# Second-level Strassen for one product of layer 1, groups in pairs, and a planned order in a fused attention and mixture-of-experts kernel

## The chip, the cores and the metric

The kernel runs on one core of a Trainium2 chip. The metric is the device time of one execution in microseconds; lower is better. Engines are named as in the profile: PE is TensorE (matmuls; PEld is its weight loads), DVE is VectorE, ACT is ScalarE, POOL is GpSimd, SP is SyncE. PE writes its results to PSUM, eight banks of 512 fp32 columns on each of 128 partitions.

## The reference

Block-sparse attention gives x, and a mixture of eight experts, mixed by weights P that are normalised by rows and columns in turn (Sinkhorn), works on x:

```python
x = np.ascontiguousarray(attn_out.transpose(0, 2, 1, 3)).reshape(B * S, H * D)
...
N, D, E, F = (3072, 512, 8, 1024)
...
P = np.exp(logits)
for _ in range(8):
    P /= P.sum(1, keepdims=True) + 1e-09
    P /= P.sum(0, keepdims=True) + 1e-09
    P *= N / E
out = np.zeros((N, D), dtype=np.float32)
for e in range(E):
    h = np.maximum(x @ w1[e], 0.0)
    ye = h @ w2[e]
    out += P[:, e:e + 1] * ye
```

Every expert is dense: all 3072 rows go through both layers of each of the eight experts.

## The kernel before, in words

**Three stretches.** Attention and expert 0 come first, up to about 124 us. A bridge follows (`bridge`, to about 165 us): the rest of expert 0, the Sinkhorn rounds, and the first layer of the first part of expert 1. Both are ordered by a list planner (`Plan`, lines 36 to 134): each unit has an engine, a cost, dependencies and a priority, and the planner emits, engine by engine, the unit that can start first, and among those within 0.02 the one of lowest priority value. The engines then run what was emitted in that order, waiting on semaphores. The third stretch, 165 us to the end, is a loop written out by hand (lines 1264 to 1313), and this is what the change rewrites.

**Strassen-Winograd.** Experts 1 to 7 compute both layers with seven block products in place of eight. In layer 1 the two row halves of w1 (256 each) and its two column halves are the blocks A, the halves of x (transposed) the blocks B. In layer 2 the hidden h is A and w2 is B. The sums S1 to S4 are formed of A, T1 to T4 of B, on DVE in fp16 (lines 931 to 983).

**A group** `(e, j, i)` (line 997) is one tile of layer 1: expert e, columns 512 j of each half of the 3072 rows (three values of j), hidden features 128 i of each half (four values of i). Its seven products p1 to p7 have two matmuls each, of 512 columns (line 988), and use four PSUM banks in turn: `pa` and `pb` (tag "ab", two banks) and `pg` (tag "g", two banks, so that groups overlap). ACT copies the first product into the bank of the third (seed), puts two partial sums aside (c5, c2) and applies two of the relus (r11, r21); DVE applies the other two with an added operand (c12, c22, line 938). The four results A11, A12, A21, A22 of 512 columns go to a tile `hf`, and four DVE sums s1 to s4 of 512 columns (lines 932 and 935) give S1 to S4 of the second layer in the same tile.

**A pair** `(e, j, c)` (line 1063) is one tile of layer 2: 128 rows ta of the upper half of the output and 128 rows tb of the lower half. Its seven products q1 to q7 have four matmuls of 256 columns each (line 994), and write a tile `xy` of two banks (four parts of 256 columns; two such tiles). c1 (ACT, line 1094), v5 (DVE, line 1099) and v6 (ACT, line 1106) move sums between parts. ya and yb add two parts each, times P, to `out_acc`, 512 columns in one DVE instruction (line 1124).

**The loop.** There are 84 groups and 84 pairs. Step n runs group n beside pair n - 4 (`LAG = 4`), with the products of both in a fixed mixture and the DVE and ACT work between them. The sums of the next expert's weights (`w1_sums`, `w2_sum`) and its loads on POOL's queue (`load_w1`, `load_w2`) are put at fixed steps. The four first groups are in the bridge; the four last pairs form a hand-written tail, two of whose pairs use the "ab" and "g" banks and add in halves of 256 columns (`y_half`, `x_half`).

Of the kernel before, what the change touches and what calls it, by code (L numbers as in the profile page):

```python
# [19 lines left out]
class Unit:  # L20
# [3 lines left out]
    def __init__(self, eng, cost, fn, deps, prio, opens, lag, shape=None):  # L24
        self.eng = eng if isinstance(eng, dict) else {eng: cost}
        self.shape = shape
        self.fn, self.deps, self.prio, self.opens, self.lag = fn, deps, prio, opens, lag
        self.start = self.end = self.on = None

# [6 lines left out]
class Plan:  # L36
# [22 lines left out]
    def order(self):  # L59
# [26 lines left out]
        while waiting or left:  # L86
# [51 lines left out]
def kernel(  # L138
# [778 lines left out]
    if True:  # L917
# [7 lines left out]
        steps = [(e, j) for e in range(1, E) for j in range(NJ)]  # L925
# [71 lines left out]
        def group(e, j, i):  # L997
            h = hs[e, j, i] = fast.tile([128, 7, 512], FP16, tag="hf", name="hf", bufs=8)
            B = {}

            def p1():
                B["a"] = fps.tile([128, 512], FP32, tag="ab", name="pa", bufs=2)
                product1(e, i, j, B["a"], "A11", "B11", True)

            def seed():
                B["g"] = fps.tile([128, 512], FP32, tag="g", name="pg", bufs=2)
                nc.scalar.copy(out=B["g"][:], in_=B["a"][:])  # L1007

            def p5():
                B["b"] = fps.tile([128, 512], FP32, tag="ab", name="pb", bufs=2)  # L1010
                product1(e, i, j, B["b"], "S1", "T1", True)

            def c5():
                B["c5"] = fast.tile([128, 512], FP32, tag="c5", name="c5", bufs=1)
                nc.scalar.copy(out=B["c5"][:], in_=B["b"][:])  # L1015

            def p6():
                product1(e, i, j, B["g"], "S2", "T2", False)

            def c2():  # L1020
                B["c2"] = fast.tile([128, 512], FP32, tag="c2", name="c2", bufs=1)
                nc.scalar.copy(out=B["c2"][:], in_=B["g"][:])  # L1022

            def p2():
                product1(e, i, j, B["a"], "A12", "B21", False)

            def r11():
                relu("ACT", h[:, A11, :], B["a"][:])

            def p3():  # L1030
                product1(e, i, j, B["b"], "S4", "B22", False)

            def c12():
                relu_plus(h[:, A21, :], B["b"][:], B["c2"][:])

            def p7():
                product1(e, i, j, B["g"], "S3", "T3", False)

            def c22():
                relu_plus(h[:, A22, :], B["g"][:], B["c5"][:])  # L1040

            def p4():
                product1(e, i, j, B["g"], "A22", "T4", False)

            def r21():
                relu("ACT", h[:, A12, :], B["g"][:])

            def s1():
                plus(h[:, S1, :], h[:, A21, :], h[:, A22, :])

            def s3():
                sub(h[:, S3, :], h[:, A11, :], h[:, A21, :])

            def s2():
                sub(h[:, S2, :], h[:, S1, :], h[:, A11, :])

            def s4():
                sub(h[:, S4, :], h[:, A12, :], h[:, S2, :])

            return {f.__name__: f for f in (p1, seed, p5, c5, p6, c2, p2, r11, p3, c12, p7, c22, p4,  # L1060
                                            r21, s1, s3, s2, s4)}

        def pair(e, j, c, spare=False, c1_at=None, tail=False):
            def h(q):
                return lambda f: hs[e, j, f][:, q, :]
# [3 lines left out]
            def part(*ks):  # L1069
                if not spare:  # L1070
                    return B["x"][:, ks[0]:ks[-1] + 1:max(1, ks[-1] - ks[0]), :]
                t, k = B["xy"[ks[0] // 2]], ks[0] % 2
                return t[:].rearrange("p (k d) -> p k d", k=2)[:, k:k + 1, :]

            def at(k):
                return part(k)[:, 0, :]

            def scale0():
                for t in (ta, tb):
                    nc.scalar.activation(out=out_acc[:, t, :], in_=out_acc[:, t, :], func=AF.Copy,  # L1080
                                         scale=P_sb[:, t, 0:1])

            def q1():
                if spare:
                    nc.gpsimd.tensor_scalar_mul(out=P_sb[:, tb, 0:1], in0=P_sb[:, tb, e:e + 1], scalar1=-1.0)
                    B["x"] = fps.tile([128, 512], FP32, tag="ab", name="px", bufs=2)
                    B["y"] = fps.tile([128, 512], FP32, tag="g", name="py", bufs=2)
                else:
                    B["x"] = xps.tile([128, 4, DH], FP32, tag="xy", name="xy", bufs=2)
                product2(e, c, at(0), h(A11), "B11", True)  # L1090

            def c1():
                B["c1"] = c1_at if c1_at is not None else fast.tile([128, DH], FP32, tag="c1", name="c1", bufs=1)[:]
# [26 lines left out]
            def add(t, k, *src):  # L1120
                src = part(*src)
                w = src.shape[1]
                acc = out_acc[:, t, k * DH:(k + w) * DH].rearrange("p (h d) -> p h d", h=w)
                nc.vector.scalar_tensor_tensor(out=acc, in0=src, scalar=P_sb[:, t, e:e + 1], in1=acc,  # L1124
# [16 lines left out]
            def fin():  # L1141
                if e == E - 1:
                    between(out_acc[:, tb, 0:DH], out_acc[:, tb, DH:DM], out_acc[:, tb, 0:DH])
                    store(tb)
# [4 lines left out]
            def y_half():  # L1149
                s3 = fast.tile([128, DH], FP32, tag="y3", name="y3", bufs=1)  # L1150
                nc.scalar.activation(out=s3[:], in_=at(3), func=AF.Copy, scale=P_sb[:, ta, e:e + 1])
                add(tb, 1, 2)
                store(tb, slice(DH, DM))
                nc.vector.scalar_tensor_tensor(
                    out=out_acc[:, tb, 0:DH], in0=at(2), scalar=P_sb[:, tb, 0:1],
                    in1=out_acc[:, tb, 0:DH], op0=ALU.mult, op1=ALU.add)
                nc.gpsimd.tensor_tensor(out=out_acc[:, ta, DH:DM], in0=out_acc[:, ta, DH:DM], in1=s3[:], op=ALU.add)

            def x_half():
                add(ta, 0, 0)  # L1160
                store(ta, eng=nc.scalar)
                nc.vector.scalar_tensor_tensor(
# [4 lines left out]
            return {f.__name__: f for f in (scale0, q1, c1, q5, v5, q6, v6, q2, q7, q3, q4, ya, yb, fin, ahead, y_half, x_half)}  # L1167

        def bridge():
            t = [fps.tile([128, 512], FP32, tag="g", name="allg", bufs=2) for _ in range(2)]  # L1170
# [6 lines left out]
            for n in range(8):  # L1177
# [26 lines left out]
                for eng, us, fn, o, w in (("DVE", 0.62, rows, (), ()), ("POOL", 0.7, by_rows, (), ()),  # L1204
                                          ("DVE", 0.48, columns, (), ()), ("PE", 0.12, totals, [buf], ()),
                                          ("DVE", 0.2, inverse, (), [buf]), ("POOL", 0.7, by_columns, (), ())):
                    step = add(eng, us, fn, [step], -50.0, opens=o, uses=w, lag=0.7 if fn is columns else 0.0)

            X, Wt = {}, {}
# [6 lines left out]
            for i in range(4):  # L1216
                for n in range(4):
                    Wt[i, n] = add("DVE", 0.3, lambda i=i, n=n: w1_sum(1, i, n), [Wt.get((i, n - 1)), U["w1n", i]],
                                   980.0 + 5 * i + n)
            step2 = None  # L1220
            for n in range(4):
                step2 = add("DVE", 0.62, lambda n=n: w2_sum(1, n),
                            [step2] + [U["pj", halves[-2], c] for c in range(HG)] + [U["w2n"]], PW + 0.01 * n)
            for i in range(4):
                f = made[1, 0, i] = group(1, 0, i)
                a, b, g = Buffer("ab"), Buffer("ab"), Buffer("g")
                k5, k2 = Buffer("c5"), Buffer("c2")
                d = {}

                def op(name, eng, us, deps, opens=(), uses=()):  # L1230
                    d[name] = add(eng, us, f[name], [d[x] if isinstance(x, str) else x for x in deps],
                                  1000.0 + PRI[i], opens=opens, uses=uses)

                op("p1", "PE", 0.44, [U["w1n", i]], [a])
                op("seed", "ACT", 0.58, ["p1"], [g], [a])
                op("p5", "PE", 0.44, ["p1", Wt[i, 0], X[0, 0]], [b])
# [130 lines left out]
```

## Time and profile before

| | us |
|---|---|
| median of 3 runs | 670.81 (670.65 to 671.78) |
| the profiled execution | 671.95 |
| its span | 670.2 |
| PE busy in 300 to 400 us | 99.92 of 100 |
| DVE busy in 300 to 400 us | 81.49 of 100 |
| ACT busy in 300 to 400 us | 56.72 of 100 |
| first q1 of the loop on PE, start | 164.87 |
| last p4 of the loop on PE, start | 651.21 |
| last instruction on DVE, start | 665.97 |

The page gives for each engine the busy time, its share of the span and the number of instructions. A line of the timeline gives the start and the length in us, the engine, the line of the kernel, the operation, output and input tiles with their shapes, a count of merged instructions, and in brackets the idle time of the engine just before it and what ended that. A matmul's length is longer than the distance to the next one, since matmuls are pipelined; distances between starts are what tells PE's pace. The other engines' instructions overlap a little too.

### The profile page before, as it was taken

The page shows a single profiled execution, that of the slowest core. Times are in us where ns is not written, and L with a number is a line of the kernel's source. Part 1 is how long each engine was busy: PE and PEld are TensorE (multiplying, and loading weights), DVE is VectorE, ACT ScalarE, POOL GpSimd, SP SyncE. Part 2 cuts the span into 40 slices and gives each one's busy share as a digit, 9 for nine tenths or more (in the row PEclk, how much of TensorE's full clock was granted, in tenths as well). Part 3 has the DMA queues.
Part 4 walks back from the last instruction along what each step waited for, and adds up shares of the span by engine and source line. Part 5 has one row for each costly group of instructions (what it writes and reads, how often), then busy time and mean ns, then how long its engine had stood idle before and what let it go on. Part 6 is the DMA issues. An engine that isn't in the chain of part 4 may idle for free.

```text
span 670.2 us, 13349 instructions
## 1 busy us (share of the span) xinstructions
PE 659.3 (98%) x5077; PEld 435.6 (65%) x5077; DVE 549.5 (82%) x1308; ACT 399.6 (60%) x781; POOL 132.4 (20%) x179
## 2 busy tenths in 40 slices
PE   7999999999999999999999999999999999999996
PEld 4666656555666666666666666666666666666665
DVE  7879998775888877888788878887789778987885
ACT  5776766566777765655565556555655565556551
POOL 8599504223001010201010010101020101100001
PEclk9999999999999999999999999999999999999999
DMA  9999958600513050502331051305040132201224
GB/s 161 183 148 146 138 84 85 83 1 2 78 16 33 1 79 1 49 1 40 41 32 16 1 79 17 33 1 79 1 41 9 30 50 24 25 2 56 87 79 158
DMA packets 124032, 36.74 MB, mean 55 GB/s; under 512 B 110144, under 2 KB 121152, under 8 KB 123968
## 3 DMA queue, kind: packets, MB, share of 16 engines
q0 software_dynamic: 104128, 25.93, 40.9%
q1 hardware_dynamic: 18880, 9.22, 6.2%
q8 instruction: 40, 0.66, 0.4%
q10 hardware_dynamic: 960, 0.74, 0.3%
q14 instruction: 24, 0.20, 0.1%
HBM read 52.45 MB, written 6.29 MB: 88 GB/s over the span
## 4 chain that ended last, share of the span: by engine, by line
PE 91%; DVE 5%; DMA 1%; ACT 1%; issue 1%; DVEq 0%; ACTq 0%
PE xy L994 37%; PE pg L988 16%; PE pb L988 11%; PE pa L988 11%; PE yps L233 5%; PE hps L223 5%; DVE xs L549 1%; DMA vx<-in_v_dram 1%; PE sg L385 1%; PE tkq L351 1%; PE ss L472 1%; PE tx L556 1%; PE vs L395 0%; DVE km L379 0%; PE py L994 0%
## 5 line engine op out<-in xcount | busy, mean ns | idle before, releaser
L994 PEld LDWEIGHTS <-hf 128*128 128x128 f16 x2352 | 230.1, 98 | 96.3 <-issue 1.6
L994 PE MATMUL xy<-w,hf 128*128 128x256 f16 x1312 | 183.4, 273 | 0.1
L994 PE MATMUL xy<-ws,hf 128*128 128x256 f16 x984 | 147.6, 273 | 0.2
L214 ACT ACTIVATE hf<-pg 128x512 f16<-128x512 f32 x84 | 50.2, 597 | 150.7 <-PE pg L988 150.7
L1124 DVE SCALAR_TENSOR_TENSOR out_acc<-xy,P_sb,out_acc 128x512 f32<-128x512 f32 x164 | 115.2, 744 | 2.4 <-PE xy L994 2.2
L932 DVE TENSOR_TENSOR hf<-hf 128x512 f16<-128x512 f16 x252 | 99.4, 421 | 9.5 <-ACT hf L214 1.1
L988 PE MATMUL pa<-xT,w 128*128 128x512 f16 x336 | 99.9, 379 | 0.0
L988 PEld LDWEIGHTS <-w 128*128 128x128 f16 x672 | 65.8, 98 | 43.8 <-issue 0.3
L938 DVE CUSTOM_DVE_ANT_0 hf<-pb,c 128x512 f16<-128x512 f32 x84 | 58.0, 691 | 40.4 <-PE pb L988 36.6
L199 POOL DMA_DIRECT2D w<-in_moe_w_dram x56 | 41.8, 758 | 220.6 <-PE pg L988 192.4
L988 PEld LDWEIGHTS <-ws 128*128 128x128 f16 x504 | 49.3, 98 | 24.9
L935 DVE TENSOR_TENSOR xy<-xy,c 128x256 f32<-128x256 f32 x82 | 35.5, 433 | 33.7 <-PE xy L994 32.8
L1022 ACT COPY c<-pg 128x512 f32<-128x512 f32 x84 | 49.2, 586 | 22.7 <-PE pg L988 22.7
L938 DVE CUSTOM_DVE_ANT_0 hf<-pg,c 128x512 f16<-128x512 f32 x84 | 57.2, 680 | 0.7 <-PE pg L988 0.7
L214 ACT ACTIVATE hf<-pa 128x512 f16<-128x512 f32 x84 | 50.6, 602 | 1.3 <-PE pa L988 1.3
L1007 ACT COPY pg<-pa 128x512 f32<-128x512 f32 x84 | 47.9, 570 | 4.7
L988 PE MATMUL pg<-xTs,w 128*128 128x512 f16 x168 | 50.0, 379 | 0.1
L988 PE MATMUL pb<-xT,ws 128*128 128x512 f16 x168 | 50.0, 379 | 0.0
L988 PE MATMUL pg<-xT,w 128*128 128x512 f16 x168 | 50.0, 379 | 0.0
L988 PE MATMUL pb<-xTs,ws 128*128 128x512 f16 x168 | 50.0, 379 | 0.0
L988 PE MATMUL pg<-xTs,ws 128*128 128x512 f16 x168 | 50.0, 379 | 0.0
L1015 ACT COPY c<-pb 128x512 f32<-128x512 f32 x84 | 49.7, 592 | 0.2 <-ACT pg L1007 0.2
(150 smaller groups left out, 796.2 us busy)
## 6 DMA issues: line engine op xcount, KB each, us to landing
w<-in_moe_w_dram POOLq DMA_DIRECT2D x8, 1024.0 KB, 9.2
w<-in_moe_w_dram POOLq DMA_DIRECT2D x56, 128.0 KB, 3.5
out_dram<-out_acc SPq DMA_DIRECT2D x20, 256.0 KB, 2.0
vx<-in_v_dram POOLq DMA_DIRECT2D x16, 192.0 KB, 6.2
qst<-in_q_dram POOLq DMA_DIRECT2D x31, 96.0 KB, 5.3
kst<-in_k_dram POOLq DMA_DIRECT2D x24, 96.0 KB, 5.4
w<-in_moe_w_dram POOLq DMA_DIRECT2D x2, 512.0 KB, 9.4
Ve<-vx SPq DMA_DIRECT2D x48, 10.2 KB, 4.1
```

The source lines that it names most:

```text
L199: nc.gpsimd.dma_start(out=t[:, :, h, :], in_=moe_w1[e].rearrange("(dk p) f -> p dk f", p=128)[:, :, f:f + 128])
L214: nc.scalar.activation(out=out, in_=in_, func=AF.Relu, bias=0.0, scale=1.0)
L223: nc.tensor.matmul(hp[:, 0:n], lhsT=w1s[e][:, dk, 128 * f:128 * (f + 1)], rhs=xT[:, dk, t0:t0 + n], start=(dk == 0), stop=(dk == KD - 1))
L932: nc.vector.tensor_tensor(out=out, in0=in0, in1=in1, op=ALU.subtract)
L935: nc.vector.tensor_tensor(out=out, in0=in0, in1=in1, op=ALU.add)
L938: nc.vector._custom_dve(TENSOR_ADD_SAT, out=out, in0=in0, in1=in1, s0=FLT_MAX, s1=0.0)
L988: nc.tensor.matmul(bank[:], lhsT=w[:, dk, :], rhs=x[:, dk, :], start=start and dk == 0, stop=dk == KH - 1, skip_group_check=True)
L994: nc.tensor.matmul(bank, lhsT=a(f)[:, 128 * c:128 * (c + 1)], rhs=w[:, f, :], start=start and f == 0, stop=f == FH - 1, skip_group_check=True)
L1007: nc.scalar.copy(out=B["g"][:], in_=B["a"][:])
L1015: nc.scalar.copy(out=B["c5"][:], in_=B["b"][:])
L1022: nc.scalar.copy(out=B["c2"][:], in_=B["g"][:])
L1124: nc.vector.scalar_tensor_tensor(out=acc, in0=src, scalar=P_sb[:, t, e:e + 1], in1=acc, op0=ALU.mult, op1=ALU.add)
```

## The change

Three things are changed together, from the end of the attention on.

**Second level for p1.** Two neighbouring groups i = 2u and 2u + 1 become a duo. Their two p1 products (A11 x B11 for 128 features each) together are a product of 256 x 256 by 256 x 512, and are computed by seven pieces m1 to m7 of one matmul with 256 columns each, in the two banks a0 and a1. Two half copies on ACT (sd, c5s) and two joins on DVE (j1, j2) combine them. The sums for it are new: `wa_sum`, four of 128 columns for each duo of an expert, and `xa_sum`, four of 256 columns for each j, once. From (e, j) = (1, 2) on all duos are split; those before keep p1 whole.

**Groups in pairs.** A duo has one `hf` tile of 7 x 2 x 512, and s1 to s4 are one instruction of 1024 columns for both groups. The second layer's tile of two banks becomes two tiles x and y of one bank each, and ya and yb become four adds y0 to y3 of 256 columns, one for each part.

**A planned order.** The hand-written loop and tail are replaced by the planner. `feed(n)` adds the units of a duo, of two pairs two duos back, and the weight loads and sums; priorities come from a table `PR` of one number per kind of unit, plus 100 for each duo. A unit now also waits, in the plan, for all earlier users of its PSUM banks on other engines. PSUM has the same eight banks: two "ab", two "g", two "x", two "y".

```diff
@@ Plan.order
                     t = max([t0, free.get(e, 0.0)]
-                            + [d.end + d.lag + hop(d, e) for d in u.deps])
+                            + [d.end + d.lag + hop(d, e) for d in u.deps]
+                            + [x.end + x.lag + hop(x, e) for b in u.banks for x in b.users
+                               if x.start is not None and x.on != e])
...
+        def moving1a(what, j):
+            t = slice(256 * j, 256 * (j + 1))
+            if what in ("T1", "T2", "T4"):
+                return xa["T1 T2 T4".split().index(what)][:, t]
+            o = 512 * j + (256 if what in ("B12", "T3", "B22") else 0)
+            return xT[:, int(what in ("B21", "B22")), o:o + 256]
...
+        def weight1a(what, e, u):
+            if what in ("S1", "S2", "S4"):
+                return wa[e, u][:, "S1 S2 S4".split().index(what), :]
+            return w1s[e, 2 * u + int(what in ("A21", "S3", "A22"))][:, int(what in ("A12", "A22")), 0, :]
...
-        def group(e, j, i):
-            h = hs[e, j, i] = fast.tile([128, 7, 512], FP16, tag="hf", name="hf", bufs=8)
...
+        def duo(e, j, u):
...
+            def piece(bank, lo, a, b, start=False):
+                nc.tensor.matmul(B[bank][:, lo:lo + 256], lhsT=weight1a(a, e, u), rhs=moving1a(b, j),
+                                 start=start, stop=True, skip_group_check=True)
+            def m1():
+                B["a0"] = psum("ab")
+                piece("a0", 0, "A11", "B11", True)
+            def sd():
+                B["a1"] = psum("ab")
+                nc.scalar.copy(out=B["a1"][:, 0:256], in_=B["a0"][:, 0:256])
+            def m5():
+                piece("a0", 256, "S1", "T1")
+            def c5s():
+                B["m5"] = single("m5", (128, 256), late)
+                nc.scalar.copy(out=B["m5"][:], in_=B["a0"][:, 256:512])
+            def m2():
+                piece("a0", 0, "A12", "B21")
+            def m6():
+                piece("a1", 0, "S2", "T2")
+            def j1():
+                plus(B["a0"][:, 256:512], B["a1"][:, 0:256], B["m5"][:])
+            def m3():
+                piece("a0", 256, "S4", "B22")
+            def m7():
+                piece("a1", 0, "S3", "T3")
+            def j2():
+                plus(B["a1"][:, 256:512], B["a1"][:, 0:256], B["m5"][:])
+            def m4():
+                piece("a1", 0, "A22", "T4")
...
             def s1():
-                plus(h[:, S1, :], h[:, A21, :], h[:, A22, :])
+                plus(h(S1), h(A21), h(A22))
...
-            def ya():
-                add(ta, 0, 0, 3)
...
-            def yb():
-                add(tb, 0, 1, 2)
...
+            def add_to(t, k, src):
+                acc = out_acc[:, t, k * DH:(k + 1) * DH]
+                nc.vector.scalar_tensor_tensor(out=acc, in0=at(src), scalar=P_sb[:, t, e:e + 1], in1=acc,
                                                op0=ALU.mult, op1=ALU.add)
...
+            def y0():
+                add_to(ta, 0, 0)
+            def y1():
+                add_to(tb, 0, 1)
+            def y2():
+                add_to(tb, 1, 2)
+            def y3():
+                add_to(ta, 1, 3)
...
+        us = dict(m=0.1092, p=0.4316, q=0.4368, seed=0.49, c5=0.49, c2=0.49, r=0.49, c12=0.607, c22=0.607, s=0.6,
+                  c1=0.275, v6=0.275, v5=0.34, y=0.665, half=0.275, join=0.34, w1=0.205, w2=0.6, wa=0.14, x=0.6,
+                  xa=0.2, sc=0.62, part=0.34)
+        LAGS = {"ACT": 0.06, "DVE": 0.04}
...
+                op("m1", "PE", us["m"], w[0] + begin + split, [a[0]])
+                op("sd", "ACT", us["half"], ["m1"], [a[1]], [a[0]])
+                op("m5", "PE", us["m"], ["m1"] + t(0), (), [a[0]])
+                op("c5s", "ACT", us["half"], ["m5"], [k5], [a[0]])
+                op("m2", "PE", us["m"], ["sd"], (), [a[0]])
+                op("m6", "PE", us["m"], ["sd"] + t(1), (), [a[1]])
+                op("j1", "DVE", us["join"], ["m6", "c5s"], (), [*a, k5])
+                op("m3", "PE", us["m"], ["j1"] + t(3), (), [a[0]])
+                op("m7", "PE", us["m"], ["j1"] + t(2), (), [a[1]])
+                op("j2", "DVE", us["join"], ["m7"], (), [a[1], k5])
+                op("m4", "PE", us["m"], ["j2"] + w[1], (), [a[1]])
...
-        for n in range(LAG, len(groups)):
...
+                op("y0", "DVE", us["v5"], ["q2"] + old[:1], (), [bx], p=PR["yd"])
+                op("y1", "DVE", us["v5"], ["q4"] + old[1:], (), [bx], p=PR["yd"] + .1)
+                op("y2", "DVE", us["v5"], ["q7"] + old[1:], (), [by], p=PR["yd"] + 2)
+                op("y3", "DVE", us["v5"], ["q3", "y0"] + old[:1], (), [by], p=PR["yd"] + 2.1)
...
+        AHEAD = 3
+        for n in range(2, 2 + AHEAD):
+            feed(n)
+        nxt = 2
+        for u in plan.order():
+            if u.fn is not None:
+                u.fn()
+            if nxt + AHEAD < len(duos) + 2 and (nxt >= len(duos) or u is made[duos[nxt]]["p51"]):
+                feed(nxt + AHEAD)
+                nxt += 1
```

In the planner's units the products, copies and relus of the two groups of a duo carry the group's number at the end: p30 and p31, c120 and c121.

More of the change, by code (lines that the diff above doesn't have):

```diff
@@ L28, in __init__ @@
         self.start = self.end = self.on = None
+        self.banks = []
 class Buffer:
@@ L1067, in pair @@
             B = {}
[L1069 to L1073, printed above, removed]
-            def at(k):
[L1076 to L1081, printed above, removed]
+            def at(k):
+                return B["xy"[k // 2]][:, k % 2 * DH:(k % 2 + 1) * DH]
@@ L1203, in bridge @@
                 buf = Buffer("k")
[L1204 to L1209, printed above, removed]
+                for eng, cost, fn, o, w in (("DVE", 0.62, rows, (), ()), ("POOL", 0.7, by_rows, (), ()),
+                                            ("DVE", 0.48, columns, (), ()), ("PE", 0.12, totals, [buf], ()),
+                                            ("DVE", 0.2, inverse, (), [buf]), ("POOL", 0.7, by_columns, (), ())):
+                    step = add(eng, cost, fn, [step], -50.0, opens=o, uses=w, lag=0.7 if fn is columns else 0.0)
             for j in range(2):
@@ L1253 @@
-        groups = [(e, j, i) for e, j in steps for i in range(4)]
-        LAG = 4
-        made, PRI, PW = {}, (5.05, 5.5, 6.05, 6.5), 1007.0
+                W2[1, n] = add("DVE", 0.62, lambda n=n: w2_sum(1, n),
+                               [W2.get((1, n - 1))] + [U["pj", halves[-2], c] for c in range(HG)] + [U["w2n"]],
+                               1007.0 + 0.01 * n)
+            for u in range(2):
+                made[1, 0, u] = plan_duo(1, 0, u, lambda name, u=u: 1000.0 + (5.05, 6.05)[u] + 0.45 * (name[-1] == "1"),
+                                         None, [made[1, 0, 0]["p51"]] if u else [], [],
+                                         {(i, n): WT[1, i, n] for i in range(4) for n in range(4)},
+                                         [X[0, n] for n in range(4)], add)
@@ L1256 @@
+        X, XA, WT, W2, WA, made, ws1, ws2, hs, wa = ({} for _ in range(10))
         bridge()
@@ L1330 @@
-        for n, d in enumerate(last):
-            if n == 1:
-                C["q6"]()
-                C["v6"]()
-            for nm in (("q2", "q4", "q3", "q7", "ya", "yb", "fin"),
-                       ("q7", "q3", "y_half", "q2", "q4", "x_half"))[n % 2]:
-                d[nm]()
+        late = ctx.enter_context(tc.tile_pool(name="late", bufs=1, side="right"))
+        xa = [late.tile([128, NH // 2], FP16, name=f"xa{n}") for n in range(3)]
+        plan.more({"x": 2, "y": 2, "c1": 1, "m5": 1})
@@ new lines, with weights, w_sums @@
+        PR = {
[8 rows of a table added]
+        }
+        QO = dict(q1=0, c1=.1, q5=.2, v5=.3, q6=.4, v6=.5, q2=.6, q4=.7, q7=.8, q3=.9)
+        duos = [(e, j, u) for e in range(1, E) for j in range(NJ) for u in range(2)]
+        pairs = {}
+        def weights(e, i, deps):
+            load(("w1", e, i), lambda: load_w1(e, i), 0.85, 1.3, deps)
+        def w_sums(e, i, prio, old=()):
+            for n in range(4):
+                WT[e, i, n] = put("DVE", us["w1"], lambda n=n: w1_sum(e, i, n),
+                                  [WT.get((e, i, n - 1)), U["w1", e, i], *old], prio + 0.01 * n)
@@ new lines, in wa_sums, with w2_sums @@
+        def wa_sums(e, u, prio, old=()):
+            for n in range(4):
+                U["wa", e, u, n] = put("DVE", us["wa"], lambda n=n: wa_sum(e, u, n),
+                                       [U.get(("wa", e, u, n - 1)), *old]
+                                       + [WT[e, 2 * u + k, 2] for k in range(2)], prio + 0.01 * n)
+        def w2_sums(e, ns, prio, old=()):
+            for n in ns:
+                W2[e, n] = put("DVE", us["w2"], lambda n=n: w2_sum(e, n),
+                               [W2.get((e, n - 1)), U["w2", e], *old], prio + 0.01 * n)
@@ new lines, in xa_sums, with users, pair_users @@
+        def xa_sums(j, prio, old=()):
+            for n in range(4):
+                XA[j, n] = put("DVE", us["xa"], lambda n=n: xa_sum(j, n), [XA.get((j, n - 1)), X[j, 0], *old],
+                               prio + 0.01 * n)
+        def users(e, j, u, names=()):
+            d = made.get((e, j, u), {})
+            return [d[x] for x in d if not names and x[0] in "mp" or x in names]
+        def pair_users(e, j, names=("q1", "q2", "q3", "q4", "q5", "q6", "q7")):
+            return [pairs[e, j, c][q] for c in range(4) for q in names] if (e, j, 0) in pairs else []
```

399 lines of the change are left out of this document (244 added, 155 removed), and 8 rows, old and new, of the table PR.

## The prediction

> **What bounds the kernel now.** I read the page first: the busy rows, the clock, the chain that ended last.
>
> ```profile
> PE 659.3 (98%) x5077; PEld 435.6 (65%) x5077; DVE 549.5 (82%) x1308; ACT 399.6 (60%) x781; POOL 132.4 (20%) x179
> PEclk9999999999999999999999999999999999999999
> PE 91%; DVE 5%; DMA 1%; ACT 1%; issue 1%; DVEq 0%; ACTq 0%
> ```
>
> PE has work for 98% of the span, at full clock, and holds 91% of the chain. A busy PE need not be at its peak, so the second view is the timeline of one step of the repeating loop.
>
> ```profile
> 300.38 0.60 PE L994 MATMUL xy<-ws,hf 128*128 128x256 f16 x4
> 300.82 0.59 PE L988 MATMUL pg<-xTs,ws 128*128 128x512 f16 x2
> 301.09 0.43 DVE L935 TENSOR_TENSOR xy<-xy,c 128x256 f32<-128x256 f32 x1 [0.38 <-PE xy L994]
> 301.43 0.42 DVE L932 TENSOR_TENSOR hf<-hf 128x512 f16<-128x512 f16 x1
> ...
> 302.12 0.59 PE L988 MATMUL pb<-xT,ws 128*128 128x512 f16 x2
> 302.55 0.59 PE L988 MATMUL pg<-xT,w 128*128 128x512 f16 x2
> 302.85 0.69 DVE L938 CUSTOM_DVE_ANT_0 hf<-pb,c 128x512 f16<-128x512 f32 x1 [0.41 <-PE pb L988]
> 303.46 0.68 DVE L938 CUSTOM_DVE_ANT_0 hf<-pg,c 128x512 f16<-128x512 f32 x1
> 304.70 0.76 DVE L932 TENSOR_TENSOR hf<-hf 128x512 f16<-128x512 f16 x2
> 305.38 1.40 DVE L1124 SCALAR_TENSOR_TENSOR out_acc<-xy,P_sb,out_acc 128x512 f32<-128x512 f32 x2
> 305.60 0.59 PE L988 MATMUL pa<-xT,w 128*128 128x512 f16 x2
> 305.80 0.37 ACT L1094 COPY c<-xy 128x256 f32<-128x256 f32 x1 [0.28 <-PE xy L994]
> ...
> 311.67 0.59 PE L988 MATMUL pa<-xT,w 128*128 128x512 f16 x2
> ```
>
> p1 starts at 305.60 and again at 311.67: a step is 6.07 us for 14 products, 0.434 each, and every product starts where the one before ends (300.38, 300.82; 302.12, 302.55). PE is saturated, so fewer columns are worth their time and a wait costs its time. The bracketed idle on DVE and ACT shows them waiting for PE, never the reverse. The last view is the tail, the one place where PE waits and where half-width adds run.
>
> ```profile
> 652.52 0.60 PE L994 MATMUL px<-w,hf 128*128 128x256 f16 x4
> 652.76 0.37 ACT L1094 COPY c<-xy 128x256 f32<-128x256 f32 x1 [0.32 <-PE xy L994]
> 653.19 0.60 PE L994 MATMUL xy<-ws,hf 128*128 128x256 f16 x4
> 662.03 0.47 DVE L1124 SCALAR_TENSOR_TENSOR out_acc<-px,P_sb,out_acc 128x256 f32<-128x256 f32 x1
> 662.42 0.47 DVE L1162 SCALAR_TENSOR_TENSOR out_acc<-px,P_sb,out_acc 128x256 f32<-128x256 f32 x1
> ```
>
> q5 at 653.19 writes columns that the copy c1 does not read, in the bank that c1 reads, and starts 0.05 after c1 ends: a bank is handed over whole. PE was ready at 652.95 and stood 0.24.
>
> **The change, part by part.** The sum is made against the profiled execution: 671.95, of which 670.2 is the span; the median shown is 670.81, so I add the difference to the median.
>
> *Fewer columns.* A duo (two groups) loses two p1 (2 x 0.434) and gains seven pieces of 256 columns, a quarter of a product each (7 x 0.1085 = 0.76): 0.108 less. Expert 1, j = 0 and 1, stays whole, so 42 - 4 = 38 duos: **-4.1 us**. The order of the changed program has these 266 pieces.
>
> *ACT.* Two half copies per duo (sd, c5s) at 0.37. ACT is busy 57 of 100 us between 300 and 400, so 0.74 in 12.1 fits; I price it at nothing, and what it can cost is in the waits below.
>
> *DVE.* By distances from start to start: s sums 0.34 (0.76 for two, less one of 0.42); the relu adds 0.61 (302.85 to 303.46); v5 0.34 (301.09 to 301.43); the full-width add 0.66 (1.40 less one of 0.74); the half-width add 0.39 (662.03 to 662.42). A sum of 1024 columns lasts 0.685 in the w2 sums (L932); less the same 0.08 of overlap, 0.60. Per duo: 8 x 0.34 of s sums become 4 x 0.60 (-0.32); 4 x 0.66 of adds become 8 x 0.39 (+0.48); two joins like v5 (+0.68); the wa sums of 128 columns have no row: between 0 and the 0.20 of the 256-column sum, on the line through 512 and 256 columns 0.14, four for three duos (+0.19). DVE gets 1.03 more per duo. It is busy 81.5 of 100 us in that stretch, 9.9 of 12.15; it becomes 10.9 of 12.04, about 91%. It still is not the bound, but its queue has little slack.
>
> *The order.* The planner puts each PE product where it holds the inputs to be just ready, with the half adds priced as 0.34 (`us["v5"]`). So I added up the emitted order at two duos in the middle. Release costs from the rows: PE to a reader with one wait 0.20 (305.60 to 305.80), with two 0.30 (302.55 to 302.85), reader to PE 0.05.
> First duo, from the end of the second group's p3: DVE runs c12 0.61, c22 0.61, v5 0.34, s1 0.60, v5 0.34, j1 0.34, s3 0.60, then y0, which ends 0.47 later; with 0.30 and 0.05 the next q4 may start at 4.26. PE has until then 6 pieces and 8 products, 0.65 + 3.47 = 4.12: 0.14 late. It is late because q4 writes the bank that y0 reads. Further on, y0 (0.39), j2 0.34, s2 0.60, two adds 0.39 each, s4 0.60, a weight sum 0.20 and y2 (0.47) end at 7.17 with the 0.05; q3, which waits for DVE, comes up on PE after q4, m4 and five products, 6.83, with the first delay 6.97: 0.20 late again. Together 0.34.
> Second duo: c12, c22, v5, y0, s1, j1, s3, y1 are 3.88, j2 ends 0.43 later; m4 may start at 4.66, and PE gets there after 6 pieces and 10 products, 4.99: 0.33 to spare, nothing lost.
> What waits behind a late q4 or q3 is all of PE, the in-order engine that sets the end. The mean of the two duos is 0.17; ends 0 and 0.34. Forty planned duos: **+6.8** (0 to 13.6). A PE delay also gives DVE time, which is why I don't go above 0.34.
> [...]
>
> *Start.* The one-time sums of x and w1 for the second level (12 of 256 columns at 0.20, 8 of 128 at 0.14) put 3.6 us on DVE into the first steps, beside x_sum, w2 sums and the ACT scalings. Before, DVE idled there 4.00 us ahead of its first v5 at 166.87, which can hide them whole. Bounds 0 to 2 (half of them exposed); I take **+1.0**.
>
> *Loads and end.* POOL issues the same w1 and w2 loads, in an order by due times; a w1 tile lands in 3.5 us and its first user is about a duo, 12 us, later. One step of the old loop (262.78 to 269.12) is 0.26 longer than two starts should be; if that goes, **-0.3**, if it comes at each of six experts, +1.6. The tail has the same products; y's of half width end it as before: 0, between -0.5 (its two gaps of 0.24 and 0.30) and +1.
>
> Sum: -4.1 + 6.8 + 1.0 - 0.3 = +3.4 us, 674.2 from the median.
>
> **The rivals.**
> *The planner's margins hold* (not slower). Its prices for the relu adds (0.607), v5 (0.34) and the full sums (0.60) are the rows' distances; the half add alone is off by 0.05. If DVE enters each duo early enough to absorb 0.4, as the second duo has 0.33 to spare, the steady loss is near nothing: -4.1 + 1.0 - 0.3 = -3.4, 667.4. It decides when the mean loss per duo falls below (4.1 + 0.3 - 1.0) / 40 = 0.085. For it: that spare time; DVE at 91% is not full. Against: the first duo, where DVE has no idle from c12 to y2.
> *A draw.* Mean loss between 0.05 and 0.12: the saving is paid back by the waits, 669.5 to 672.2.
> *DVE sets the pace.* All duos lose 0.34 or a little more, where delayed y adds delay the next duo's c12 and the bank that p5 needs: -4.1 + 13.6 + 1.0 = +10.5, 681.3. For it: no step catches up when DVE stays busy; against: the second duo.
> *The change does not do what it says.* All 266 pieces are in the emitted order; no chance.
>
> **How the numbers follow.** Forecast, slower by 1.4 to 7: 0.50. DVE sets the pace: 0.07. Margins hold: 0.33. Draw: 0.10. A measurement of this kernel tells 0.2%, 1.3 us, from no change; so slower 0.57, same 0.10, faster 0.33. The time is the forecast's, 674.2, with 672.2 to 678 as its own range. The 8-in-10 range must reach most of the faster case and a part of the slowest: 667 to 679.
>
> **What would show it.** Right: in the changed profile, between 250 and 600 us, PE idle of 0.1 to 0.3 a duo, named as waiting for DVE at L996 (q4, q3 on px, py) or L1040 (m4); half adds near 0.47 in pairs 0.39 apart; DVE near 90%. Columns right: 266 matmuls at L1040. Wrong: duos of 12.04 to 12.1 us with DVE idle ahead of c12; or PE waiting for ACT instead (sd ahead of m6, r11 ahead of p5), which I price at nothing; or for a weight load.

## The result and the profile after

| | before | after |
|---|---|---|
| median, us | 670.73 (670.63 to 671.78, 4 runs) | 679.34 (678.24 to 679.68, 4 runs) |
| span of the profiled execution, us | 670.2 | 677.7 |
| the profiled execution, us | 671.95 | 679.68 |

The changed kernel takes 1.0122 times as long, with a 95% interval of 1.0104 to 1.0139: 8.6 us slower. The forecast was 3.4 us slower, with 667 to 679 us as the range. From the page of the changed kernel, these are the busy rows, the clock in 40 slices, the shares of the chain that ended last, and the large w2 loads with their time from issue to landing:

```profile
PE 664.1 (98%) x5191; PEld 446.7 (66%) x5191; DVE 573.5 (85%) x1447; ACT 420.8 (62%) x858; POOL 133.4 (20%) x179
...
PEclk9999999999899999999999999999999999999999
...
PE 70%; DVE 23%; issue 2%; DMA 2%; ACT 2%; DVEq 0%; ACTq 0%
...
w<-in_moe_w_dram POOLq DMA_DIRECT2D x8, 1024.0 KB, 9.0
```

DVE held 5% of the chain before and holds 23% now: PE waits for it in many places. One slice of the clock row is an 8, where before all were 9. To see where the time is lost, I read the windows. Columns are the window, its length, the busy time (and count) of PE, PEld, DVE, ACT and POOL, the granted TensorE clock, the DMA share and GB/s. Before:

```profile
160.00:180.00 20.00, 20.00 (x129) 12.49 (x128) 11.93 (x25) 13.21 (x27) 3.14 (x5) 1.00 0.49 66
200.00:600.00 400.00, 399.70 (x2759) 269.68 (x2758) 334.07 (x710) 231.61 (x473) 38.41 (x52) 1.00 0.24 29
```

The same two windows after, then three short ones inside the first:

```profile
160.00:180.00 20.00, 17.11 (x93) 9.55 (x91) 12.80 (x35) 12.92 (x25) 3.34 (x4) 0.91 0.50 66
200.00:600.00 400.00, 398.87 (x2844) 277.12 (x2842) 350.74 (x816) 243.18 (x525) 38.54 (x52) 1.00 0.25 29
...
173.00:174.00 1.00, 0.00 (x0) 0.00 (x0) 0.40 (x1) 0.00 (x0) 0.00 (x0) 1.00 1.74 174
...
177.00:178.00 1.00, 1.00 (x6) 0.58 (x4) 1.00 (x3) 1.00 (x3) 0.00 (x0) 0.50 0.00 0
178.00:179.00 1.00, 1.00 (x7) 0.69 (x6) 0.76 (x2) 0.96 (x2) 0.00 (x0) 0.50 0.00 0
```

There are two losses. The first sits in one place: between 160 and 180 us PE stands for 2.89 us, and then runs at a granted clock of 0.50 for some 3.4 us (176.42 to 179.83). The second is spread over the loop and hardly shows in these sums (1.13 us idle in 400, against 0.30), because a matmul's length as recorded (0.59) is longer than the pace at which they follow each other (0.434 for a product): a wait below about 0.16 us disappears in that overlap. The distances between starts show it. I added, over all matmuls from 164 us to the end, what each distance exceeds 0.216 us for 512 columns or 0.109 for 256:

```
us lost on PE against its pace    before   after
160 to 180 us                        0.0     4.9
from 180 us to the end               1.7     8.5
```

The changed kernel loses 13.4 us to gaps where the one before lost 1.7. With the 4.1 us of columns that it no longer multiplies, that makes 13.4 - 1.7 - 4.1 = 7.6 us, and the spans differ by 7.5. So the ledger closes for the two profiled executions. The one of before (671.95) is about 1 us above the median of its kernel, so the medians differ by 8.6. Of the 8.5, about 2.3 stand ahead of q3, 1.5 ahead of q4, 2.2 ahead of p3, 1.3 ahead of the pieces m (L1040), and the rest ahead of p5, p6 and others.

The timeline of the changed kernel shows both losses, the first loss down to 178.94, and a duo in mid-loop from 332.99. Columns: start, length, engine, line, operation, tiles, count, and in brackets the idle time just before on that engine with what ended it.

```profile
164.56 0.94 POOL L213 DMA_DIRECT2D w<-in_moe_w_dram  x1 [1.41 <-PE yps L236]
...
166.85 0.21 DVE L934 TENSOR_TENSOR wa<-w,wa 128x128 f16<-128x128 f16 x1
168.70 0.43 DVE L937 TENSOR_TENSOR py<-px,c 128x256 f32<-128x256 f32 x1 [1.64 <-PE px L996]
...
171.47 0.60 PE L996 MATMUL px<-w,hf 128*128 128x256 f16 x4
173.60 0.69 DVE L934 TENSOR_TENSOR ws<-w 128x1024 f16<-128x1024 f16 x1 [3.42 <-DMA w<-in_moe_w_dram]
174.21 0.68 DVE L940 CUSTOM_DVE_ANT_0 hf<-pg,c 128x512 f16<-128x512 f32 x1
174.95 0.59 PE L990 MATMUL pg<-xTs,w 128*128 128x512 f16 x2 [2.88 <-DVE hf L940]
177.24 1.91 PE L996 MATMUL px<-ws,hf 128*128 128x256 f16 x8
178.94 1.04 PE L990 MATMUL pab<-xT,w 128*128 128x512 f16 x2
...
332.99 0.68 DVE L940 CUSTOM_DVE_ANT_0 hf<-pg,c 128x512 f16<-128x512 f32 x1
...
333.75 0.59 PE L990 MATMUL pg<-xTs,w 128*128 128x512 f16 x2
333.76 0.59 ACT L1099 COPY c<-pab 128x512 f32<-128x512 f32 x1 [0.66 <-DVE hf L940]
334.39 0.59 PE L990 MATMUL pab<-xT,ws 128*128 128x512 f16 x2
...
338.59 0.60 PE L996 MATMUL px<-w,hf 128*128 128x256 f16 x4
338.60 0.48 DVE L1215 SCALAR_TENSOR_TENSOR out_acc<-px,P_sb,out_acc 128x256 f32<-128x256 f32 x1
339.12 0.60 PE L996 MATMUL px<-ws,hf 128*128 128x256 f16 x4
```

*The first loss.* The load of expert 2's w2 is issued at 164.56. The planner prices it at 5.0 us after 0.9 of issue (the code of the load: `0.9, 5.0`). With the lags that it adds to every load (lines 676 to 678), and 0.1 for each step from one engine or queue to the next, it holds the data ready 7.5 us after the issue begins, and places the first sum of this w2 where it holds the load to be there, at the head of DVE's queue, ahead of a relu add (c22). But the load lands at 173.58, 9.02 us after its issue. That explains 1.5 of the 3.42 us that DVE waits for it. Most of the rest is the start of the issue: the row at 164.56 shows POOL idle for 1.41 us until the last layer-2 product of expert 0 (yps, L236) is done, and the plan does not know this wait, since for expert 2 the list of products that the load must follow, `pair_users(e - 1, 2)`, is empty. The relu add behind that sum, which has no need of w2, starts at 174.21, and p4, which needs the relu add's bank, starts at 174.95, 2.88 us after PE ran dry. The clock falls after that: the eight matmuls at 177.24 take 1.70 us to the next start, where eight of the same form at 184.59, at a clock of 1.00, take 0.87. The granted clock in the short windows makes up for 1.7 us, and 2.9 + 1.7 is nearly all of the 4.9.

*The second loss.* At 339.12 a q4 starts 0.04 after the half add of 338.60 ends, while PE was ready at 339.03: 0.1 late, for the bank that this add reads. The other form is at 334.39, where p3 is 0.2 late. It waits for the ACT copy c5 to read its bank, which ends at 334.35; c5 itself starts late, after 0.66 us of idling, because DVE's relu add of 332.99 has to end first (333.67). ACT is the engine named there, DVE is the cause. The waits of the whole execution (engine, line, what it waited for; us in total, times, longest) say the same:

```profile
ACT c L1099 <- DVE hf L940: 19.6, 30, 2.9
...
DVE ws L934 <- DMA w<-in_moe_w_dram: 3.4, 1, 3.4
```

c5's wait for DVE comes 30 times; the wait for the load comes once in the whole kernel.

### The profile page after: what moved, and what is told of

It reads as the page before. It is cut to its first block, busy times and chain, and to the rows that moved or that the text cites. A ratio compares the mean times of both kernels' runs of the same rounds, so it can differ in the third digit from the quotient of the medians.

```text
span 677.7 us, 13610 instructions
## 1 busy us (share of the span) xinstructions
PE 664.1 (98%) x5191; PEld 446.7 (66%) x5191; DVE 573.5 (85%) x1447; ACT 420.8 (62%) x858; POOL 133.4 (20%) x179
## 4 chain that ended last, share of the span: by engine, by line
PE 70%; DVE 23%; issue 2%; DMA 2%; ACT 2%; DVEq 0%; ACTq 0%
PE px L996 16%; PE pab L990 12%; PE pg L990 12%; PE py L996 10%; DVE out_acc L1215 6%; PE yps L236 5%; PE hps L226 5%; PE pab L1040 3%; DVE hf L940 3%; DVE hf L934 3%; DVE ws L934 2%; DVE pab L937 1%; DMA w<-in_moe_w_dram 1%; DVE xs L552 1%; DVE hf L937 1%
## 5 line engine op out<-in xcount | busy, mean ns | idle before, releaser
L996 PEld LDWEIGHTS <-hf 128*128 128x128 f16 x2352 | 230.1, 98 | 86.2 <-issue 3.4
L996 PE MATMUL px<-w,hf 128*128 128x256 f16 x656 | 97.9, 273 | 0.0
L996 PE MATMUL px<-ws,hf 128*128 128x256 f16 x656 | 96.1, 274 | 0.0
L996 PE MATMUL py<-w,hf 128*128 128x256 f16 x656 | 93.4, 272 | 0.7 <-DVE out_acc L1215 0.4
L217 ACT ACTIVATE hf<-pab 128x512 f16<-128x512 f32 x84 | 50.2, 599 | 68.2 <-PE pab L990 50.4
L934 DVE TENSOR_TENSOR hf<-hf 128x1024 f16<-128x1024 f16 x126 | 85.7, 681 | 0.4 <-ACT hf L217 0.3
L1215 DVE SCALAR_TENSOR_TENSOR out_acc<-py,P_sb,out_acc 128x256 f32<-128x256 f32 x164 | 75.2, 474 | 2.7 <-PE py L996 2.6
L1215 DVE SCALAR_TENSOR_TENSOR out_acc<-px,P_sb,out_acc 128x256 f32<-128x256 f32 x164 | 74.4, 474 | 2.1 <-PE px L996 2.1
L940 DVE CUSTOM_DVE_ANT_0 hf<-pab,c 128x512 f16<-128x512 f32 x84 | 57.7, 686 | 21.5 <-PE pab L990 17.7
L990 PE MATMUL pab<-xT,w 128*128 128x512 f16 x184 | 54.8, 382 | 0.0
L990 PE MATMUL pab<-xT,ws 128*128 128x512 f16 x168 | 50.0, 379 | 0.6
```

Of the source, the lines that this page charges most:

```text
L217: nc.scalar.activation(out=out, in_=in_, func=AF.Relu, bias=0.0, scale=1.0)
L934: nc.vector.tensor_tensor(out=out, in0=in0, in1=in1, op=ALU.subtract)
L940: nc.vector._custom_dve(TENSOR_ADD_SAT, out=out, in0=in0, in1=in1, s0=FLT_MAX, s1=0.0)
L990: nc.tensor.matmul(bank[:], lhsT=w[:, dk, :], rhs=x[:, dk, :], start=start and dk == 0, stop=dk == KH - 1, skip_group_check=True)
L996: nc.tensor.matmul(bank, lhsT=a(f)[:, 128 * c:128 * (c + 1)], rhs=w[:, f, :], start=start and f == 0, stop=f == FH - 1, skip_group_check=True)
L1215: nc.vector.scalar_tensor_tensor(out=acc, in0=at(src), scalar=P_sb[:, t, e:e + 1], in1=acc, op0=ALU.mult, op1=ALU.add)
```

## The experiments

Theory: two of the planner's prices are wrong, and PE pays for both. The 1 MB load of w2 is priced at 5.0 us and takes 9.0 from issue to landing; the half add is priced at 0.34 (`us["v5"]`) and costs 0.39 from start to start. Each makes DVE later than planned where the order has no slack. Rivals: the second level itself costs what it saves (more DVE work and more bank hand-overs, in any order); the merged sums of 1024 columns hold up DVE; or the half adds, wherever they stand, collide with the products on their banks.

**The load's price.**

```diff
-                        load(("w2", e + 1), lambda: load_w2(e + 1), 0.9, 5.0, pair_users(e - 1, 2))
+                        load(("w2", e + 1), lambda: load_w2(e + 1), 0.9, 9.0, pair_users(e - 1, 2))
```

> One number changed in the changed kernel: the planner's duration of a w2 load, 5.0 becomes 9.0, which is what the profile shows from issue to landing. Theory (the start: a w2 sum stood at the head of DVE's queue while its load was on the way, PE lost 4.9 us between 160 and 180 us and the clock fell there): that loss falls to about 1, the rest stays, 675 to 676 us. Rival (the start is slow because of the one-time sums on DVE, which stay): no change, 678.5 to 680.

Measured: 674.41 us, 1.0054 [1.0039, 1.0069] of before, so 4.9 us less than the changed kernel, and a little below the 675 that I had expected at best, since nothing of the first loss is left. The windows of this run:

```profile
160.00:180.00 20.00, 20.00 (x127) 12.31 (x126) 15.98 (x44) 17.58 (x36) 3.35 (x4) 1.00 0.49 66
200.00:600.00 400.00, 399.20 (x2837) 276.40 (x2835) 349.69 (x813) 242.32 (x523) 36.77 (x48) 1.00 0.24 29
```

PE is busy for all of the 20 us in which it stood, at a clock of 1.00, and the load is no faster (9.10 us from issue to landing): only the sum that needs it comes later (179.16 in place of 173.60). The gaps of this run are 8.9 us in sum, all of them after 180 us. So this one number removes the first loss, and the second is left. It is not the load's true price: with 9.0 the plan holds the data ready 11.5 us after the issue begins, 2.4 more than the load takes here, and this surplus covers the wait of the issue that the plan does not know.

**The half add's price, on top of that.**

```diff
+                  xa=0.2, sc=0.62, part=0.34, yh=0.39)
...
-                op("y0", "DVE", us["v5"], ["q2"] + old[:1], (), [bx], p=PR["yd"])
+                op("y0", "DVE", us["yh"], ["q2"] + old[:1], (), [bx], p=PR["yd"])
```

and the same for y1, y2 and y3.

> The same, and the half-width adds y0 to y3 priced at 0.39 in the planner in place of 0.34. Nothing else: the same instructions in another order. Theory (the steady loss of 8.5 us on PE is DVE falling behind a plan that is 0.4 us per duo too short): most of the loss goes, 667 to 670.5 us. Rival (the loss is the price of more hand-overs of a PSUM bank between engines, whatever the order): 673.5 to 675.5, as without the price.

Measured: 667.40 us, 0.9951 [0.9936, 0.9966] of before; 7.0 less than the run with the load's price alone. It executes the same units, in another order; the gaps fall from 8.9 us to 1.7, as many as the kernel before had. From this run's page, windows and timeline:

```profile
PE 655.7 (99%) x5191; PEld 446.7 (67%) x5191; DVE 575.1 (86%) x1447; ACT 422.6 (63%) x858; POOL 133.4 (20%) x179
```

```profile
160.00:180.00 20.00, 20.00 (x127) 12.19 (x125) 15.84 (x43) 17.28 (x34) 3.35 (x4) 1.00 0.50 66
200.00:600.00 400.00, 399.88 (x2886) 281.98 (x2885) 356.66 (x825) 248.27 (x531) 36.39 (x48) 1.00 0.24 29
```

```profile
306.21 0.47 DVE L1215 SCALAR_TENSOR_TENSOR out_acc<-px,P_sb,out_acc 128x256 f32<-128x256 f32 x1
...
307.03 0.60 PE L996 MATMUL px<-w,hf 128*128 128x256 f16 x4
...
307.47 0.60 PE L996 MATMUL px<-ws,hf 128*128 128x256 f16 x4
...
308.12 0.60 PE L996 MATMUL px<-ws,hf 128*128 128x256 f16 x4
308.14 0.48 DVE L1215 SCALAR_TENSOR_TENSOR out_acc<-px,P_sb,out_acc 128x256 f32<-128x256 f32 x1
...
308.56 0.60 PE L996 MATMUL py<-w,hf 128*128 128x256 f16 x4
308.86 0.87 DVE L1215 SCALAR_TENSOR_TENSOR out_acc<-px,P_sb,out_acc 128x256 f32<-128x256 f32 x2
```

PE, DVE and ACT have the same instruction counts as after (5191, 1447, 858), and DVE is even busier in its share. The rows are two pairs of one step. The y0 of the first runs at 306.21 and is done 0.8 us before the q4 on its bank (307.47); the q4 of the second (308.12) is emitted ahead of its y0 (the first of the two adds at 308.86). The add of 308.14 is a y1 of the first pair, on the other x bank. So no q4 here starts just behind an add, and products follow each other at their pace (307.03, 307.47; 308.12, 308.56). DVE's amount of work was not the cause; where it was late was.

**The half add's price without the load's.** The second edit alone, load back at `0.9, 5.0`.

> The half adds priced at 0.39, the w2 load at 5.0 again: the second correction without the first. Theory (two independent losses, 4.9 at the start and 7.0 in the steady part): 4 to 5 us above the kernel with both, 671 to 672.5 us, with PE standing near 170 to 180 us behind a w2 sum that waits for its load. Rival (the start loss belonged to the late DVE): 667 to 668.5.

Measured: 672.68 us, 1.0023 [1.0013, 1.0034]: 5.3 more than with both edits, where the load's edit gave 4.9 alone (4.8 by the ratios, each taken against the kernel before in its own set of runs). I had expected 672.5 at most. The two losses are separate and add up. The window of 160 to 180 us is that of the changed kernel again:

```profile
160.00:180.00 20.00, 17.29 (x94) 9.48 (x93) 12.68 (x35) 12.92 (x25) 3.33 (x4) 0.91 0.48 66
```

**The half adds behind the products on their banks.** On top of the load's price, adds still priced at 0.34; y0 must now follow q4, and y2 must follow q3.

```diff
-                op("y0", "DVE", us["v5"], ["q2"] + old[:1], (), [bx], p=PR["yd"])
+                op("y0", "DVE", us["v5"], ["q2", "q4"] + old[:1], (), [bx], p=PR["yd"])
...
-                op("y2", "DVE", us["v5"], ["q7"] + old[1:], (), [by], p=PR["yd"] + 2)
+                op("y2", "DVE", us["v5"], ["q7", "q3"] + old[1:], (), [by], p=PR["yd"] + 2)
```

> The w2 load priced at 9.0, the half adds still at 0.34, but y0 is put behind q4 and y2 behind q3 in the plan, so that no product of a pair waits for an add that reads its bank. Rival (the hand-overs between q4, q3 and the adds are the loss, some 4.8 us): they vanish, 670 to 671 us. Theory (DVE is late in its queue, and PE meets that lateness at whichever product comes next): part of it shows at other products (q1 behind y3, p4 behind c22), 672 to 674 us.

Measured: 672.47 us, 1.0026 [1.0015, 1.0037]: 1.9 less than with the load's price alone. The gaps at q4 and q3 go, but 5.0 us of gaps are left, at p4, at q6 and in the tail. With the adds still priced too low, DVE is late somewhere else. The hand-overs that I had named were places where the lateness came out, not its cause.

**Without the second level, in the good order.** The two prices mended, every p1 whole, and no sums for the pieces.

```diff
-                if (e, j) >= (1, 2):
+                if False:
```

> As the second kernel (w2 load 9.0, half adds 0.39), but no duo is split: p1 stays whole, and the sums of the second level are left out. PE has 4.1 us more of products, DVE about 0.9 us less per duo. Theory (with right prices the second level is worth its columns): 4 us above the second kernel, 671 to 674.5 us. Rival (the pieces' waits eat their columns: m6 behind sd, m4 behind j2): the same as the second kernel within 1 us.

Measured: 670.98 us, 1.0002 [0.9993, 1.0012]. Its gaps are 1.5 us, about those of the run with both prices mended, so the difference between the two, 3.6 us, is what the second level is worth when nothing waits; 4.1 was the sum of its columns. The rest of the change (pairs of groups, merged sums, half adds, planner) is worth nothing measurable by itself: without the second level it stands where the hand-written loop stood.

**The merged sums taken apart**, with both prices mended.

```diff
-                plus(h(S1), h(A21), h(A22))
+                for k in range(2):
+                    plus(h(S1, k), h(A21, k), h(A22, k))
```

and so for s2 to s4, priced at 0.68 for the two.

> The kernel with both prices, but each of s1 to s4 is two instructions of 512 columns again, priced together at 0.68: DVE gets 0.32 us per duo more, 13 us in all. Theory (DVE at some 87% of the span has room for it if the plan knows it): within 1.5 us of the kernel with both, 667 to 669 us. Rival (the merged sums are what makes the second level possible, DVE has no room left): 671 us or more.

Measured: 667.86 us, 0.9948 [0.9933, 0.9963], against 0.9951 [0.9936, 0.9966] with merged sums. The merge makes no difference that these runs can tell, and it is not what held DVE up.

**Other prices for the half add**, load's price mended, only the number changed: 0.365 and 0.44 in one set of runs, 0.38, 0.40 and 0.41 in another.

> The half adds priced at 0.365, between the changed kernel's 0.34 and the profile's 0.39; w2 load 9.0. Theory (the loss is what the plan is too short by, 8 times the error per duo): about half of the 7 us, 669.5 to 672.5 us. Rival (the good order at 0.39 is one lucky draw of a sensitive planner): anything from 667 to 676, without order.

> The half adds priced at 0.44, too dear by as much as 0.34 was too cheap. Theory (a plan that is too long leaves DVE early and costs PE little): 667 to 669.5 us. Rival (a lucky draw): 671 us or more, as likely as not.

> The half adds priced at 0.38, w2 load 9.0. Theory (from 0.34, 674.4, through 0.365, 671.4, to 0.39, 667.4, time follows the error of the price): 667 to 669.5 us. Rival (0.39 is a lucky order): outside that.

> The half adds priced at 0.40. Theory: 667 to 669 us, as at 0.39. Rival (a lucky order): 670 us or more, as 0.44 gave.

> The half adds priced at 0.41. Theory: between the kernels at 0.39 and 0.44, 667 to 670 us. Rival (a lucky order): no order in the times.

| price of the half add, us | median, us | ratio to before | gaps of PE in the trace, us | gaps of PE in the plan, us |
|---|---|---|---|---|
| 0.34 | 674.41 | 1.0054 [1.0039, 1.0069] | 8.9 | 2.7 |
| 0.365 | 671.43 | 1.0006 [0.9995, 1.0017] | 5.1 | 2.1 |
| 0.38 | 667.00 | 0.9946 [0.9929, 0.9962] | 1.2 | 0.4 |
| 0.39 | 667.40 | 0.9951 [0.9936, 0.9966] | 1.7 | 1.2 |
| 0.40 | 667.35 | 0.9952 [0.9937, 0.9966] | 1.7 | 1.2 |
| 0.41 | 667.76 | 0.9958 [0.9943, 0.9973] | 2.4 | 2.0 |
| 0.44 | 670.22 | 0.9987 [0.9978, 0.9997] | 4.4 | 5.1 |

The gaps in the trace are counted from 180 us on. The last column is the time for which the planner itself leaves PE idle from the first q1 of the loop on, by the starts and ends that its code gives to the units; before 180 us these gaps are nothing.

From 0.38 to 0.41 the time is flat within the intervals, around the 0.39 that the trace shows. Below, it rises as the price departs from the trace. The last two columns separate two causes. What the trace loses beyond the plan is lateness, and it follows the price: 6.2 us at 0.34, 3.0 at 0.365, 0.4 to 0.8 from 0.38 to 0.41. What the plan itself leaves idle belongs to the order and goes from 0.4 to 5.1. With one order for each price, these runs can't tell whether that part is a draw, so there the rival of a lucky order is not refuted. Of the 7.2 us of gaps that go between 0.34 and 0.39, 5.7 are lateness and 1.5 are of this kind. The priorities (`PR`) were the same in all runs; others would give other orders, and none was tried.

At 0.44 I had expected little loss, and it costs 2.8 us over 0.39. That run has 4.4 us of gaps, 3.6 of them ahead of q6, which waits for DVE's v5. Here DVE is not late: the plan holds these gaps too, 3.9 us ahead of q6. At the five largest, 2.7 us together in the plan, it puts v5 behind the s1 of 1024 columns. One of them in the trace:

```profile
330.12 0.69 DVE L937 TENSOR_TENSOR hf<-hf 128x1024 f16<-128x1024 f16 x1
...
330.72 0.43 DVE L937 TENSOR_TENSOR py<-px,c 128x256 f32<-128x256 f32 x1
...
331.20 0.60 PE L996 MATMUL py<-ws,hf 128*128 128x256 f16 x4 [0.23 <-DVE py L937]
```

In the changed kernel the v5 stands ahead of the s1 at the same place (336.39 and 336.72).

The version with the price of 0.38 is the fastest that was run, 3.7 us below the kernel before; 0.38, 0.39 and 0.40 can't be told apart.

## Why the prediction was wrong in size

*Direction.* Slower was right, and the cause given for it (half adds priced at 0.34 that cost 0.39) is the one that the experiments confirm for the loop. The time was 679.3 where 674.2 was forecast and 679 was the upper end.

*The step that failed: start and loads.* The prediction put +1.0 on the start, between 0 and 2, for the one-time sums of x and w1, and -0.3 on the loads, since POOL issues "the same w1 and w2 loads" and a w1 tile lands in 3.5 us, well ahead of its use. The start measured 4.9. The one-time sums were not its cause: twelve of the twenty are done at 167.06, and DVE then idles 1.64 us until PE gives it work at 168.70; the other eight come at 179.59 and later, behind the stop; and the run with the load's price alone has all twenty and no gap before 180 us. Cover was there, as the prediction said. What cost the time was a load that it did not price, and PE waiting for a weight load, here by way of DVE, is the last of its own signs of being wrong. The page of before lists the w2 loads of 1 MB beside those of w1, at 9.2 us from issue to landing, and the new code prices them at 5.0. The prediction looked at the small load's row alone. And "the same loads" was true of the issue (165.33 before, 164.56 after) but not of the use: the hand-written loop makes the first sum of w2 at a fixed step far behind the load (191.87, where the load landed at 174.32), the planner as soon as it believes the load to be there. With 4.9 in place of 1.0 the sum of the prediction is +7.3, or 678.1; most of the rest is that the profiled execution of before lies about 1 us above its median.

*A part with no term at all: the clock.* 1.7 of the 4.9 us are not waiting but slow matmuls after it, at a granted clock of 0.50. The sum held no such term.

*Columns, -4.1.* Right. All 266 pieces run, the ledger closes with 4.1, and the run without the second level gives 3.6.

*Waits in the loop, +6.8 (0 to 13.6).* Right in size: 8.5 us of gaps after 180 us, less the 1.7 that the kernel before has too. That it agrees to the decimal is luck: the prediction had two duos, 0.34 and 0, and took the mean for forty, and some 2.3 of the 8.5 are gaps that the plan itself leaves. The places were half right. I added up q4 and q3, which hold some 3.8 of the 8.5; p3, the pieces, p5 and p6 hold most of the rest.

*DVE near 91%.* It is 85.9 of 100 us between 300 and 400 (81.5 before): the duos are longer than planned, and the share falls. In the run with both prices mended it is 87.4, so 91% was too high; why was not measured. What mattered held: DVE is not the bound. That "its queue has little slack" held for the order with the wrong price alone: with both prices mended it takes the sums taken apart as well (89.9 of 100 us) at no loss that can be told.

*Half adds.* They last 0.474 on average, and two in a row take 0.87, so 0.39 to 0.40 apart, as taken from the tail of before.

*ACT at nothing.* Right for its load (60.7 of 100 us). The prediction said that PE waiting for ACT would speak against it; PE does wait for c5 at p3, but c5 waits for DVE, as the row at 333.76 shows.

*The rivals.* "The planner's margins hold" was refuted for the kernel as changed, and its stated price, 667.4, is what the kernel gives once the two prices are mended (667.40). The agreement is partly luck, since that sum holds 1.0 for a start that then costs nothing. The condition that I gave for it, spare time in DVE early enough, is the wrong one. It needed no spare time, but an order made with true durations. "DVE sets the pace" (681.3) came close to the time by accident: DVE did not set the pace in the loop.

*The banks.* The prediction counted y0 ahead of q4 and y2 ahead of q3 as hand-overs of a bank. Where PE comes early the trace shows them as such: q4 at 339.12 starts 0.04 after the add ends, and two products at L996 wait 0.16 and 0.20 for an add that reads their bank (220.46, 636.90). But their number decides little. By the emitted order of the 82 pairs with half adds, the changed kernel has y0 ahead of q4 in 61 and y2 ahead of q3 in 66, and loses 3.8 us ahead of q4 and q3; the run with both prices mended has them in 51 and 48, and loses 0.5 there. Here a hand-over cost where PE got to the bank before DVE was done with it.

## What to carry to other kernels

An order made by a planner is only as good as its prices and its list of waits: before trusting it, set every price, of loads too, beside its row in a profile, since here mending 0.05 us on one kind of instruction gave 7.0 us, and mending a load that was held ready 3.4 us too early gave 4.9. Compare the idle time that the plan itself contains with the idle time in the trace: the difference points to wrong prices or waits that the plan does not know, the rest is the order. An instruction that waits for a load held up work behind it that has no need of the load (the relu add on DVE, behind a sum that waited 3.42 us), so place it late rather than as early as the load might allow. When a rewrite mixes a saving with a new order, price them apart: the saving was real (3.6 us) and the order hid it.

## What the hardware showed that I had not expected

Two stops of PE cost more than their length. After 2.88 us without a matmul the granted clock of the changed kernel stood at 0.50 for 3.413 us, from 176.42, that is 1.5 us *after* PE had started again, and cost 1.7 us more. By the clock record of this trace the stretches at 1.00 before and after it, 170.67 and 494.93 us, are 50 and 145 times as long. The run with only the half add's price mended shows it a second time (2.71 us idle, a mean of 0.91 over the same 20 us). Shorter idle times left the clock at 1.00: 0.16 to 0.38 us in the changed kernel, and 1.75 us (ending at 8.47) in the kernel before. What sets the idle time that suffices, and why the fall came 1.5 us after the restart, was not shown.
